# Crossbar transposes of K and Q issued one loop slot earlier, and stores held back for Pool's queue, in a window attention followed by a max-of-three FFN

## The chip, the cores and the metric

The kernel runs on one NeuronCore of a Trainium2 chip. The metric is the device time of one launch in microseconds. TensorE (PE) does the matmuls, VectorE (DVE), ScalarE (ACT) and GpSimd (POOL) the elementwise work, and SyncE (SP) issues most DMAs. Each engine takes its own instructions in order; so does each queue of DMA issues, SP's and Pool's among them.

## The reference

Attention over 4 batches × 8 heads × 768 positions × 64 dims: each query sees the first 4 positions (the sinks) and the last 128. Then an FFN with the elementwise maximum of three products.

```python
scores = scale * np.matmul(q, k.transpose(0, 1, 3, 2))
keep = is_sink | in_window              # n_sink = 4, window = 128
scores = np.where(keep, scores, -1e9)
a = softmax(scores)
x = np.matmul(a, v).transpose(0, 2, 1, 3).reshape(B * S, H * D)      # 3072 x 512
h = np.maximum(np.maximum(x @ w1, x @ w2), x @ w3)                   # 512 -> 768
out = h @ w_out                                                      # 768 -> 512, float32
```

## The kernel before

The work is cut into 12 chunks of 256 positions, three to a batch (c = 0, 1, 2 within it). For every chunk the kernel goes through these steps:

- **load**: three DMAs of 512 KB each (k, q, v in float32) on SP's queue, `load` (L74 to L80), into `raw` buffers of which there are 3 per tensor;
- **cast** (L488): Pool casts k and q to bfloat16 (`k_bf`, `q_bf`, two buffers each; L178) and v into `vb` (L181, four buffers);
- **transposition of K and Q**: for chunks 2 and 3 by TensorE and a copy out of PSUM (`turn`, L205), from chunk 4 on by the DMA crossbar (`turn_xbar`, L214: two DMAs for K at L217, one for Q at L220), issued on SP's queue; chunks 0 and 1 are transposed from float32 (`turn32`, L193). Results are `kT` and `qT`;
- **scores** (L516): sink scores (L254) and window scores (L279) on TensorE, exponentials on ACT (L281), masks on DVE (L287, L289);
- **attend** (L504): scores times V on TensorE (L311), normalised by DVE into `x_sb` (L317, L318), and then transposed to `xT`: by TensorE for chunks below 4 (`xpose`, L328), from then on by the crossbar with two DMAs on SP's queue (`xpose_xbar`, L337);
- **F** (`ffn_h`, L346): nine steps of 8 matmuls each (L352), copied by ACT (L356) or merged by DVE's maximum (L358);
- **y** (`ffn_y`, L360): two halves of 6 matmuls (L363), a copy by ACT (L369), and two stores each on SP's queue (L371).

The order on every engine is written out by hand. After a prologue and two slots written out (from L384 on), slot i of the loop at L574 runs, in this order: attend(i+1) with its x transposes, the casts of chunk i+2, the load of chunk i+3, four steps of F(i), the crossbar transposes of K and Q of chunk i+2, its scores, y(i−1) with its stores, the rest of F(i) between the masks. A transposition thus stands in the same slot as the scores that read it, and on SP's queue it stands behind x of chunk i+1 and the load of chunk i+3. PSUM has 8 banks that are taken in turn. The weights come in float32 and are cast by DMAs on Pool's queue (L147, L156).

Of the kernel before, what the change touches and what calls it, by code (L numbers as in the profile page):

```python
# [14 lines left out]
def kernel(  # L15
# [33 lines left out]
    KQ_XBAR = 4  # L49
    X_XBAR = 4  # L50

    with tc.manual_schedule():
# [21 lines left out]
        def load(ci, parts):  # L74
            b, c = divmod(ci, CPB)
            for t, g in parts:
                h = slice(0, H) if g is None else slice(4 * g, 4 * g + 4)
                nc.sync.dma_start(  # L78
                    out=raws[ci][t][:, h],
                    in_=dram[t][b, h, c * 256:c * 256 + 256].rearrange("h (p i) d -> p h (i d)", i=2))  # L80

        HALVES = [("k", 0), ("q", 0), ("k", 1), ("q", 1), ("v", 0), ("v", 1)]
        for ci in (0, 1):
            load_begin(ci)
            load(ci, HALVES)
# [25 lines left out]
        vb = [const.tile([128, 2, H, D + 1], BF16, name=f"vb{s}") for s in range(4)]  # L111
# [17 lines left out]
        def consts_late(eng):  # L129
            for s in range(1, 4):  # L130
                eng.memset(vb[s][:, :, :, D:D + 1], 1.0)
            for s in range(2):
                eng.memset(ks[s], 0.0)
            eng.memset(sel, 0.0)
            for h in range(2):
                for i in range(2):
                    eng.tensor_copy(sel[:, h, 4 * h + 2 * i:4 * h + 2 * i + 2],
                                    ident[:, 64 * i:64 * i + 2])
# [41 lines left out]
        def cast_v(ci, n, i, eng):  # L180
            eng.tensor_copy(vb[ci % 4][64 * i:64 * i + 64, n, :, 0:D],  # L181
                            raws[ci]["v"][64 * n:64 * n + 64, :, i])
# [49 lines left out]
        def sink_v(b, eng):  # L232
            t = bank([128, 2, D + 1], F32, "vs_ps")
            for p in range(NP):
                for h in range(2):
                    nc.tensor.matmul(t[32 * p:32 * p + 32, h], lhsT=sel[:, h],
                                     rhs=vb[(CPB * b) % 4][:, 0, 2 * p + h],
                                     start=(h == 0), stop=(h == 1), skip_group_check=True)
            eng(vs[b % 2], t)
# [53 lines left out]
        def av(ci, pairs, eng=None):  # L293
# [10 lines left out]
            for p in pairs:  # L304
                first = c == 0
                for t in range(2):
                    for s, n in ((2 * t, 2 * c + t - 1), (2 * t + 1, 2 * c + t)):
                        if n < 0:
                            continue
                        for h in range(2):  # L310
                            nc.tensor.matmul(  # L311
                                o[p][:, t, h], lhsT=es[ci, p][:, h, s],
                                rhs=vb[(CPB * b + n // 2) % 4][:, n % 2, 2 * p + h],
# [9 lines left out]
        def xT_of(ci):  # L323
            if ci not in xTs:
                xTs[ci] = work.tile([128, DS, 256], BF16, tag="xT", name="xT")
            return xTs[ci]

        def xpose(ci, g, eng):  # L328
            pt = bank([128, 2, 2, 128], BF16, "xt_ps")
            x = xs[ci].rearrange("p t h d -> p t (h d)")  # L330
            for a in range(2):
                for t in range(2):
                    ds = 2 * g + a
                    nc.tensor.transpose(pt[:, a, t], x[:, t, ds * 128:(ds + 1) * 128], ident)
            eng(xT_of(ci)[:, 2 * g:2 * g + 2], pt.rearrange("p a t c -> p a (t c)"))  # L335

        def xpose_xbar(ci):  # L337
            for t in range(2):
                nc.sync.dma_start_transpose(  # L339
                    out=xT_of(ci)[:, :, t * 128:(t + 1) * 128],  # L340
                    in_=xs[ci][:, t].rearrange("p h d -> p (h d)"))
# [4 lines left out]
        def ffn_h(ci, wi, fp):  # L346
# [3 lines left out]
            for f in range(2):  # L350
                for ds in range(DS):
                    nc.tensor.matmul(hp[:, f], lhsT=w_sb[wi, 2 * fp + f][:, ds],  # L352
                                     rhs=xTs[ci][:, ds], start=(ds == 0), stop=(ds == DS - 1))
# [5 lines left out]

        def ffn_y(ci, t, last=False):  # L360
# [4 lines left out]
            y = work.tile([128, d_model], F32, tag="y", bufs=4, name="y_sb")  # L365
            r0 = ci * 256 + t * 128
            o = out[r0:r0 + 128].rearrange("(r i) f -> i r f", i=2)
            if not last:
                nc.scalar.copy(y, yp)  # L369
                for i in range(2):  # L370
                    nc.sync.dma_start(out=o[i], in_=y[64 * i:64 * i + 64])  # L371
                return
            for i in range(2):
                ip = slice(64 * i, 64 * i + 64)
                if i:
                    nc.vector.tensor_copy(y[ip], yp[ip])
                else:
                    nc.scalar.copy(y[ip], yp[ip])
                (nc.sync, nc.scalar)[i].dma_start(out=o[i], in_=y[ip])

        V, P, A = nc.vector, nc.gpsimd, nc.scalar


        consts_dve()  # L384
        warm(8)
        turn32(0, "k", 0, V.tensor_copy)
        turn32(0, "q", 0, A.copy)
        warm(2)
        score(0, 0)
        turn32(0, "k", 1, V.tensor_copy)  # L390
        score(0, 1)
        turn32(0, "q", 1, A.copy)
        for n in range(2):
            for i in range(2):
                cast_v(0, n, i, P)
        mask(0, 0, V)
        score(0, 2)
        mask(0, 1, V)
        wait_for(raws[1]["k"][0:1, 0, 0, 0:1], P)
        load_w(0, 0, 256)  # L400
        load_w(0, 256, 256)
        load_w(0, 512, 256)
        load_w(1, 0, 256)
        turn32(1, "k", 0, V.tensor_copy)
        score(0, 3)
        turn32(1, "q", 0, V.tensor_copy)
        av(0, [0])
        mask(0, 2, V)
        av(0, [1])
        xpose(0, 0, A.copy)  # L410
        mask(0, 3, V)
        av(0, [2])
        turn32(1, "k", 1, V.tensor_copy)
        av(0, [3])
        turn32(1, "q", 1, V.tensor_copy)
        score(1, 0)
# [10 lines left out]
        mask(1, 0, V)  # L427
        ffn_h(0, 0, 0)
        score(1, 1)
        mask(1, 1, V)  # L430
# [4 lines left out]
        mask(1, 2, V)  # L435
# [3 lines left out]
        mask(1, 3, V)  # L439
        ffn_h(0, 1, 0)  # L440
        av(1, [2, 3])
        ffn_h(0, 1, 1)
        xpose(1, 0, A.copy)
        xpose(1, 1, A.copy)
        ffn_h(0, 1, 2)

        load_begin(2)
        wait_for(wts[2, 0][0:1, 0, 0:1], P)
        gate(2, "kqv", P)
        load(2, [("k", None), ("q", None), ("v", None)])  # L450
        for a in range(2):
            load_wo(a)
        for fp in range(3):
            ffn_h(1, 0, fp)
        cast_qk(2, "k", 0, P)
        cast_qk(2, "k", 1, P)
        for fp in range(3):
            ffn_h(1, 1, fp)
        for i in range(2):
            for n in range(2):  # L460
                cast_v(2, n, i, P)
        ffn_h(0, 2, 0)
        ffn_h(0, 2, 1)
        ffn_h(0, 2, 2)
        cast_qk(2, "q", 0, V)
        cast_qk(2, "q", 1, V)
        ffn_h(1, 2, 0)
        turn(2, "k", V.tensor_copy)
        turn(2, "q", A.copy)
        ffn_h(1, 2, 1)  # L470
        sink_score(2)
        for p in range(NP):
            score(2, p)
        ffn_h(1, 2, 2)
        load_begin(3)
        gate(3, "kqv", P)
        load(3, [("k", None), ("q", None), ("v", None)])
        for p in range(NP):
            mask(2, p, V)
        ffn_y(0, 0)  # L480
        ffn_y(0, 1)
        av(2, range(NP))
        ffn_y(1, 0)
        xpose(2, 0, A.copy)
        xpose(2, 1, A.copy)
        ffn_y(1, 1)

        def cast(ci):  # L488
            for t in "kq":
                for i in range(2):  # L490
                    cast_qk(ci, t, i, P)
            for n in range(2):
                for i in range(2):
                    cast_v(ci, n, i, P)

        def load_all(ci):
            if ci < NCH:
                load_begin(ci)
                load(ci, [("k", None), ("q", None), ("v", None)])

        def F(ci, n):
            ffn_h(ci, n % 3, n // 3)

        def attend(ci):  # L504
            if ci >= NCH:
                return
            av(ci, range(NP))
            if ci >= X_XBAR:
                xpose_xbar(ci)

        def T(ci):
            if ci < X_XBAR:
                xpose(ci, 0, A.copy)
                xpose(ci, 1, A.copy)

        def scores(ci):  # L516
            if ci >= NCH:
                return
            b, c = divmod(ci, CPB)
            if ci < KQ_XBAR:  # L520
                turn(ci, "k", V.tensor_copy)
                turn(ci, "q", A.copy)
            if c == 0:
                sink_k(b, V)
                sink_v(b, V.tensor_copy)
            sink_score(ci)
            for p in range(NP):
                score(ci, p)

        def masks(ci, ps_):  # L530
            for p in ps_:
                if ci < NCH:
                    mask(ci, p, V)


        cast(3)
        load_all(4)
        for n in range(5):
            F(2, n)
        scores(3)  # L540
        cast(4)
        load_all(5)
        turn_xbar(4)
        F(2, 5)
        masks(3, [0, 1])
        F(2, 6)
        masks(3, [2, 3])
        F(2, 7)
        F(2, 8)

        attend(3)
        ffn_y(2, 0)
        T(3)
        ffn_y(2, 1)
        cast(5)
        load_all(6)
        turn_xbar(5)
        scores(4)
        for n in range(3):
            F(3, n)  # L560
            masks(4, [n])
        F(3, 3)
        masks(4, [3])
        F(3, 4)
        attend(4)
        F(3, 5)
        F(3, 6)
        scores(5)
        F(3, 7)
        masks(5, [0, 1])  # L570
        F(3, 8)
        masks(5, [2, 3])

        for i in range(4, NCH):  # L574
            attend(i + 1)
            if i + 2 < NCH:
                cast(i + 2)
            load_all(i + 3)
            for n in range(4):
                F(i, n)  # L580
            if i + 2 < NCH:
                turn_xbar(i + 2)
            scores(i + 2)
            ffn_y(i - 1, 0)
            masks(i + 2, [0])
            ffn_y(i - 1, 1)
            masks(i + 2, [1])
            F(i, 4)
            masks(i + 2, [2])
            F(i, 5)  # L590
            masks(i + 2, [3])
            F(i, 6)
            F(i, 7)
            F(i, 8)
        ffn_y(NCH - 1, 0)
        ffn_y(NCH - 1, 1, last=True)
# [38 lines left out]
```

## Time and profile before

| | us |
|---|---|
| median of 3 runs | 271.96 (270.34 to 273.59) |
| the profiled execution | 271.53 |
| its span, first to last instruction | 269.6 |
| TensorE busy | 186.8 |
| VectorE, ScalarE, Pool busy | 115.1, 90.8, 64.3 |
| DMA packets of SP's queue, Pool's queue | 52.3%, 8.1% of 16 engines over the span |
| bytes moved | 34.92 MB |

How to read it: "busy" is the sum of the durations of an engine's instructions; the page also cuts the span into 40 slices and gives the busy share of each as a digit (9 is 90% or more), and beside it the granted TensorE clock in tenths. In the views, a line like `L217 SPq DMA_TRANSPOSE kT<-k_bf` is source line, queue or engine, operation, output and input. The chain of waits follows the last instruction back to what released each step. A wait in square brackets is the idle time of the engine before an instruction, and what ended it. Releasers are inferred from the times of the semaphores.

### The profile page before, as it was taken

The numbers are of one execution on the slowest core, as the hardware profiler recorded it, in microseconds if no ns is written. First come the engines' busy times: TensorE is split into PE (matmuls) and PEld (weight loads), VectorE is DVE, ScalarE is ACT, GpSimd is POOL, SyncE is SP. The second block draws the span as 40 slices with busy tenths as digits, with TensorE's granted clock in tenths as the row PEclk, the third lists the DMA queues.
The fourth block names the chain that finished last, engine by engine and source line by source line (L and its number), as shares of the span: only waits on it lengthen the run. The fifth ranks groups of instructions, "written<-read, shape, count | busy, mean of one in ns | idle before, by whom it ended". The sixth has DMA issues, their size and how long they took to land.

```text
span 269.6 us, 4874 instructions
## 1 busy us (share of the span) xinstructions
PE 186.8 (69%) x1934; PEld 138.2 (51%) x1946; DVE 115.1 (43%) x251; ACT 90.8 (34%) x177; POOL 64.3 (24%) x130
## 2 busy tenths in 40 slices
PE   6878999987777605940894099219903990999992
PEld 5665786774565503830483058115802580587870
DVE  4385676458186502640273028113800380283441
ACT  1528308453727105210711081015202510812221
POOL 3592223647351033005200510070015000000000
PEclk9999999999999965995599579757975798699998
DMA  6999974999892293339033903692187116034133
GB/s 185 278 147 189 199 178 122 251 264 245 216 232 43 47 254 50 80 67 282 4 78 82 270 2 78 162 190 48 38 197 148 45 40 113 0 80 93 26 78 79
DMA packets 71750, 34.92 MB, mean 130 GB/s; under 512 B 27440, under 2 KB 68656, under 8 KB 71728
## 3 DMA queue, kind: packets, MB, share of 16 engines
q1 hardware_dynamic: 67152, 31.34, 52.3%
q0 software_dynamic: 4496, 3.15, 8.1%
q8 instruction: 15, 0.25, 0.4%
q10 hardware_dynamic: 80, 0.13, 0.2%
q14 instruction: 7, 0.06, 0.1%
HBM read 25.17 MB, written 6.29 MB: 117 GB/s over the span
## 4 chain that ended last, share of the span: by engine, by line
PE 54%; DMA 25%; SPq 6%; DVE 5%; ACT 5%; issue 3%; POOL 1%; ACTq 0%; DVEq 0%; POOLq 0%
PE h_ps L352 27%; DMA q_raw<-in_q_dram 14%; PE y_ps L363 13%; DMA qT<-q_bf 10%; PE st L279 5%; SPq L339 4%; PE o_ps L311 3%; ACT e_sb L281 3%; PE kt L200 2%; PE qt L200 2%; DVE e_sb L287 2%; DVE h_sb L358 1%; DMA k_raw<-in_k_dram 1%; SPq L78 1%; SPq L217 1%
## 5 line engine op out<-in xcount | busy, mean ns | idle before, releaser
L352 PE MATMUL h_ps<-xT,w 128*128 128x256 bf16 x864 | 99.1, 273 | 1.2 <-ACT xT L335 1.1
L352 PEld LDWEIGHTS <-w 128*128 128x128 bf16 x864 | 83.5, 98 | 13.4 <-issue 2.1
L358 DVE TENSOR_TENSOR h_sb<-h_sb,h_ps 128x512 bf16<-128x512 bf16 x72 | 49.4, 686 | 54.8 <-PE h_ps L352 47.2
L281 ACT ACTIVATE e_sb<-st 128x512 bf16<-128x512 f32 (+1 forms) x96 | 45.6, 586 | 27.3 <-PE st L279 26.9
L287 DVE TENSOR_TENSOR e_sb<-e_sb,msk 128x1024 bf16<-128x1024 bf16 x32 | 21.8, 696 | 58.1 <-ACT e_sb L281 58.0
L356 ACT CAST h_sb<-h_ps 128x512 bf16<-128x512 f32 x36 | 21.2, 593 | 66.6 <-PE h_ps L352 66.6
L363 PE MATMUL y_ps<-wo,h_sb 128*128 128x512 bf16 x132 | 39.4, 438 | 1.8 <-issue 1.3
L178 POOL CAST k_bf<-k_raw 128x512 bf16<-128x512 f32 x20 | 11.9, 622 | 112.8 <-DMA k_raw<-in_k_dram 97.4
L181 POOL CAST vb<-v_raw 64x512 bf16<-64x512 f32 x48 | 30.5, 636 | 18.3 <-DMA v_raw<-in_v_dram 16.3
L279 PE MATMUL st<-qT,kT 64*128 64x128 bf16 (+1 forms) x256 | 17.7, 293 | 24.1 <-DMA qT<-q_bf 22.2
L254 PE MATMUL sk<-qT,ks 128*32 128x256 bf16 x32 | 2.8, 335 | 42.7 <-DMA qT<-q_bf 42.5
L363 PEld LDWEIGHTS <-h_sb 128*128 128x128 bf16 x144 | 15.2, 112 | 21.9 <-issue 11.9
L279 PEld LDWEIGHTS <-kT 64*128 64x128 bf16 x256 | 11.8, 117 | 28.4 <-issue 26.2
L254 PEld LDWEIGHTS <-ks 128*32 128x32 bf16 x32 | 1.1, 96 | 44.8 <-issue 42.9
L318 DVE TENSOR_TENSOR x_sb<-o_ps,rc 128x256 bf16<-128x256 f32 x48 | 20.4, 424 | 1.6
L369 ACT COPY y_sb<-y_ps 128x512 f32<-128x512 f32 x23 | 13.6, 601 | 17.7 <-PE y_ps L363 13.2
L311 PE MATMUL o_ps<-vb,e_sb 128*128 128x65 bf16 x352 | 14.9, 194 | 3.3 <-DVE e_sb L287 2.8
L258 ACT ACTIVATE e_sink<-sk 128x256 bf16<-128x256 f32 x8 | 3.1, 385 | 41.6 <-PE sk L254 41.6
L311 PEld LDWEIGHTS <-e_sb 128*128 128x128 bf16 x352 | 12.4, 97 | 5.7 <-DVE e_sb L287 3.9
L178 POOL CAST q_bf<-q_raw 128x512 bf16<-128x512 f32 x18 | 10.8, 629 | 6.4 <-DMA q_raw<-in_q_dram 6.4
L289 DVE TENSOR_TENSOR e_sb<-e_sb,msk 128x768 bf16<-128x768 bf16 x16 | 10.1, 651 | 4.6 <-ACT e_sb L281 4.6
L228 DVE COPY ks<-kT 64x16 bf16<-64x16 bf16 x8 | 2.1, 256 | 20.0 <-DMA kT<-k_bf 19.9
(59 smaller groups left out, 79.5 us busy)
## 6 DMA issues: line engine op xcount, KB each, us to landing
out_dram<-y_sb SPq DMA_DIRECT2D x47, 128.0 KB, 2.4
k_raw<-in_k_dram SPq DMA_DIRECT2D x10, 512.0 KB, 4.6
q_raw<-in_q_dram SPq DMA_DIRECT2D x10, 512.0 KB, 5.8
v_raw<-in_v_dram SPq DMA_DIRECT2D x10, 512.0 KB, 7.1
w<-in_moe_w_dram POOLq DMA_DIRECT2D x5, 256.0 KB, 5.6
k_raw<-in_k_dram SPq DMA_DIRECT2D x4, 256.0 KB, 5.2
q_raw<-in_q_dram SPq DMA_DIRECT2D x4, 256.0 KB, 5.3
v_raw<-in_v_dram SPq DMA_DIRECT2D x4, 256.0 KB, 5.4
```

The source lines that it names most:

```text
L178: eng.tensor_copy(bfs[ci, t][:, :, i], x)
L181: eng.tensor_copy(vb[ci % 4][64 * i:64 * i + 64, n, :, 0:D], raws[ci]["v"][64 * n:64 * n + 64, :, i])
L279: nc.tensor.matmul(o, lhsT=kk, rhs=qq, start=True, stop=True)
L281: nc.scalar.activation(e[:, h, lo:], st[h][:, lo:], AF.Exp, scale=scale)
L287: eng.tensor_mul(e, e, msk)
L311: nc.tensor.matmul(o[p][:, t, h], lhsT=es[ci, p][:, h, s], rhs=vb[(CPB * b + n // 2) % 4][:, n % 2, 2 * p + h], start=first, stop=(s == 2 ...
L318: nc.vector.tensor_mul(xs[ci][:, :, 2 * p:2 * p + 2], o[p][:, :, :, 0:D], rc.unsqueeze(3).to_broadcast([128, 2, 2, D]))
L352: nc.tensor.matmul(hp[:, f], lhsT=w_sb[wi, 2 * fp + f][:, ds], rhs=xTs[ci][:, ds], start=(ds == 0), stop=(ds == DS - 1))
L356: nc.scalar.copy(dst, hp)
L358: nc.vector.tensor_max(dst, dst, hp)
L363: nc.tensor.matmul(yp, lhsT=hs[ci][:, fb, t * 128:(t + 1) * 128], rhs=wo[fb // 3][:, fb % 3], start=(fb == 0), stop=(fb == FB - 1))
L369: nc.scalar.copy(y, yp)
```

## The change

- **K and Q a slot ahead.** In the loop, slot i now holds the cast of chunk i+3, the load of chunk i+4 and the transposition `KQ(i+3)`; the scores of chunk i+2 in that slot read what slot i−1 transposed. `vb` has five buffers instead of four. The slots before the loop are written out in the same manner.
- **Crossbar from chunk 5 on** (`KQ_XBAR`, `X_XBAR` 4 → 5): K, Q and x of chunk 4 are transposed by TensorE.
- **x in one DMA.** `xT` gets the layout half, block, column; one transposing DMA of 128 × 1024 takes the place of two. F reads its moving operand as two blocks of 128 columns.
- **y held.** y of a chunk is one tile of two halves, with 8 buffers instead of 4 tiles of one half. Nothing is stored before slot 7. From there Pool's queue stores, up to three chunks a slot: chunks 0 to 2, 3 to 5, 6 and 7, 8, 9. Chunk 10 and the first half of 11 go by SP, the last half by SP and ACT.
- **Prologue.** For chunk 0, two of the six half loads go by ACT's queue; v comes before the second halves of k and q. The first weights no longer wait for chunk 1's k. Load 2 waits for w2's first part instead of w3's; load 3 comes behind the cast of K of chunk 2, load 4 behind the casts of chunk 3 (`gated`: Pool writes one element of each raw tile first). 15 warming matmuls instead of 10. The steps of chunks 0 to 4 are interleaved anew.

The core of the diff:

```diff
-    KQ_XBAR = 4
-    X_XBAR = 4
+    KQ_XBAR = 5
+    X_XBAR = 5
...
-        HALVES = [("k", 0), ("q", 0), ("k", 1), ("q", 1), ("v", 0), ("v", 1)]
+        HALVES = [("k", 0), ("q", 0), ("v", 0), ("v", 1), ("k", 1), ("q", 1)]
         for ci in (0, 1):
             load_begin(ci)
-            load(ci, HALVES)
+            load(ci, HALVES, {("q", 0): nc.scalar, ("v", 1): nc.scalar} if ci == 0 else None)
...
         def xpose_xbar(ci):
-            for t in range(2):
-                nc.sync.dma_start_transpose(
-                    out=xT_of(ci)[:, :, t * 128:(t + 1) * 128],
-                    in_=xs[ci][:, t].rearrange("p h d -> p (h d)"))
+            nc.sync.dma_start_transpose(
+                out=xT_of(ci).rearrange("p t s c -> p (t s) c"),
+                in_=xs[ci].rearrange("p t h d -> p (t h d)"))
...
+        def store(ci, t, i, eng):
+            r0 = ci * 256 + t * 128
+            eng.dma_start(out=out[r0:r0 + 128].rearrange("(r i) f -> i r f", i=2)[i],
+                          in_=ys[ci][64 * i:64 * i + 64, t])
...
+        def KQ(ci):
+            if ci < NCH:
+                if ci < KQ_XBAR:
+                    turn(ci, "k", V.tensor_copy)
+                    turn(ci, "q", A.copy)
+                else:
+                    turn_xbar(ci)
...
-        warm(8)
+        warm(12)
...
-        wait_for(raws[1]["k"][0:1, 0, 0, 0:1], P)
...
-        wait_for(wts[2, 0][0:1, 0, 0:1], P)
+        wait_for(wts[1, 0][0:1, 0, 0:1], P)
...
-        for i in range(4, NCH):
-            attend(i + 1)
-            if i + 2 < NCH:
-                cast(i + 2)
-            load_all(i + 3)
+        held = 0
+        for i in range(5, NCH):
+            A_(i + 1)
+            if i + 1 < NCH:
+                xpose_xbar(i + 1)
+            cast(i + 3)
+            load_all(i + 4)
+            KQ(i + 3)
             for n in range(4):
                 F(i, n)
-            if i + 2 < NCH:
-                turn_xbar(i + 2)
             scores(i + 2)
-            ffn_y(i - 1, 0)
-            masks(i + 2, [0])
-            ffn_y(i - 1, 1)
-            masks(i + 2, [1])
+            late = i - 1 > 4
+            if late:
+                ffn_y(i - 1, 0)
+            masks(i + 2, 0)
+            if late:
+                ffn_y(i - 1, 1)
+            masks(i + 2, 1)
+            if i >= 7:
+                n = min(i - 1, held + 3) if i < NCH - 1 else i - 1
+                stores(range(held, n), P)
+                held = n
             F(i, 4)
...
+        stores(range(held, NCH - 1), nc.sync)
         ffn_y(NCH - 1, 0)
+        for i in range(2):
+            store(NCH - 1, 0, i, nc.sync)
         ffn_y(NCH - 1, 1, last=True)
```

## The prediction

> **What bounds the kernel now.** I read the page first: busy shares, then the slices.
>
> ```profile
> span 269.6 us, 4874 instructions
> PE 186.8 (69%) x1934; PEld 138.2 (51%) x1946; DVE 115.1 (43%) x251; ACT 90.8 (34%) x177; POOL 64.3 (24%) x130
> PE   6878999987777605940894099219903990999992
> PEclk9999999999999965995599579757975798699998
> ```
>
> TensorE is busy most, yet in the second half its row falls to 0 in a regular beat, and the granted clock falls with it. So one thing is missing once per slot of the loop; the view of waits names it.
>
> ```profile
> PE sk L254 <- DMA qT<-q_bf: 42.5, 6, 11.6
> PE st L279 <- DMA qT<-q_bf: 22.2, 2, 11.4
> 69.95 0.29 PE L254 MATMUL sk<-qT,ks 128*32 128x256 bf16 x4 [1.38 <-DMA qT<-q_bf]
> ```
>
> Columns: waiter, releaser, total us, times, longest. Eight waits, 64.7 us together, one for each of chunks 4 to 11, whose K and Q are transposed by the crossbar; the first, at 69.95, is still short, those from chunk 6 on are long. Why so late? SP's queue, Pool's casts and the chain over one slot (i = 6, from the views in order of time):
>
> ```profile
> 123.45 1.17 POOL L178 CAST k_bf<-k_raw 128x512 bf16<-128x512 f32 x2 [19.55 <-DMA k_raw<-in_k_dram]
> 125.16 1.17 POOL L178 CAST q_bf<-q_raw 128x512 bf16<-128x512 f32 x2 [0.55 <-DMA q_raw<-in_q_dram]
> 142.80 2.54 SPq L339 DMA_TRANSPOSE xT<-x_sb  x2
> 145.39 0.58 SPq L78 DMA_DIRECT2D k_raw<-in_k_dram  x1
> 146.02 5.57 DMA q_raw<-in_q_dram
> 147.85 3.85 SPq L217 DMA_TRANSPOSE kT<-k_bf  x2
> 151.80 1.34 SPq L220 DMA_TRANSPOSE qT<-q_bf  x1
> 155.28 0.41 PE sk L254 x3
> ```
>
> Counting loads from the start, the one at 145.39 is chunk 9's, and the transposes at 147.85 are chunk 8's, whose bf16 operands Pool had ready by 126.3. So the data was there 21 us early; what comes late is the issue, because on SP's in-order queue it stands behind x of chunk 7 (released at 142.80) and behind a load. The chain of waits puts 146.02 to 151.6 down to the landing of a q_raw; by the count that load is another chunk's. The last slot proves it: no load and no cast is left, and the wait is still there.
>
> ```profile
> 221.03 2.52 SPq L339 DMA_TRANSPOSE xT<-x_sb  x2
> 223.64 2.54 SPq L217 DMA_TRANSPOSE kT<-k_bf  x2
> 226.27 1.26 SPq L220 DMA_TRANSPOSE qT<-q_bf  x1
> 229.52 0.40 PE L254 MATMUL sk<-qT,ks 128*32 128x256 bf16 x4 [6.65 <-DMA qT<-q_bf]
> ```
>
> From x's release to the scores it takes 8.5 us without a load and 12.5 with one (142.80 to 155.28), while TensorE has four steps of F, about 3.5 us, to put beside it.
>
> **The change, part by part.** *K and Q one slot ahead.* The transposes of chunk i+3 now stand in slot i and are read in slot i+1. They still follow x and a load on SP, so they land some 12.5 us into slot i, and scores(i+3) come one slot plus 3.5 us in. With a slot of 13 us (below) that leaves 4 us; the waits go entirely. Their operands need cast(i+3), of a load issued at the head of slot i−1: the load lands in 5.6 us (146.02) and Pool has 5.4 us of work a chunk (64.3 / 12), 11 of 13 us, so SP doesn't stand there. Were it to stand, x of the next chunk and its load stand behind it. The price is one more slot of buffers (vb from 4 to 5); raw, kT and qT are freed two slots before reuse.
>
> What is late next? TensorE's own work, so I price it at full clock, from rows of the chain and of the order of time:
>
> ```profile
> 42.03 0.29 PE sk L254 x4
> 42.33 0.99 PE st L279 x24
> 46.96 0.23 PE o_ps L302 x8
> 47.18 1.10 PE o_ps L311 x32
> 49.58 0.62 PE xt_ps L334 x8
> 51.49 4.38 PE h_ps L352 x40
> 244.48 0.21 PE y_ps L363
> 244.74 2.32 PE y_ps L363 x10
> 247.07 7.86 PE h_ps L352 x72
> 264.65 0.59 ACT y_sb L378
> ```
>
> A chunk's F is 72 matmuls, 7.86; its two y 2.53 each pair (0.21 + 2.32); scores 0.29 + 0.99; attention times V 0.23 + 1.10. A full slot: 7.86 + 2.53 + 1.28 + 1.33 = 13.0 us, where the chain above shows 25 to 27. F(2, 0) begins at 51.49. What TensorE still has to do from there, after the change: F and y of chunks 2 to 11, 10 × 10.39 = 103.9; scores and AV of chunks 3 to 11, 9 × 2.61 = 23.5; x of chunks 3 and 4, 2 × 0.62; K and Q of chunks 3 and 4, 16 matmuls each.
>
> ```profile
> 40.37 0.58 PE qt L211 x7
> 128.90:134.00 5.10, 4.88 (x35) 2.46 (x37) 1.38 (x2) 4.50 (x10) 0.63 (x2) 0.50 0.01 3
> 0.00:30.00 30.00, 24.06 (x310) 17.79 (x311) 17.54 (x47) 13.15 (x26) 16.12 (x46) 1.00 1.02 194
> 30.00:51.50 21.50, 21.07 (x222) 16.07 (x224) 13.04 (x26) 10.48 (x20) 6.45 (x16) 1.00 0.82 193
> 145.30:155.30 10.00, 0.02 (x4) 0.05 (x4) 0.00 (x0) 0.00 (x0) 4.00 (x7) 0.64 0.97 223
> 160.70:165.00 4.30, 4.30 (x46) 3.68 (x45) 3.18 (x5) 1.18 (x3) 0.00 (x0) 1.00 0.53 122
> 221.00:223.60 2.60, 1.87 (x18) 1.43 (x15) 1.38 (x2) 0.59 (x1) 0.00 (x0) 1.00 0.27 53
> ```
>
> (The windows: stretch, length, PE, PEld, DVE, ACT, POOL busy, granted clock, DMA share, GB/s.) K and Q at 0.58 twice is 1.16 a chunk, 2.3. Together 130.9 us.
>
> *The clock.* After a wait of 11 us the next 5 us run at 0.50; 21.5 us without such a wait run at 1.00 (the windows at 128.90 and 30.00). Using full-clock prices already takes this gain: scores, y and the first F took 4.88 us there for what costs 2.5 to 3 at full clock, so about 2 us a slot.
>
> *Chunk 4 moved from crossbar to TensorE*: counted above; three transposes and two of x leave the DMA engines. The copies go to DVE and ACT, which have 9.6 and 7.6 us of work a chunk (115.1 and 90.8 / 12) beside 13.
>
> *x in one DMA.* Two issues of 1.26 become one. I take qT's row (the same 128 × 1024, 1.26 to issue, 3.1 to land) against 1.26 + 2.5 for two: no gain on the path, and F(i+1) reads it a slot later anyway. F's moving operand becomes two blocks of 128 instead of one of 256. The trace has no such F; the nearest, the sink scores, read Q in strides at 0.29 for four: I take nothing, with 5% of 94 us, 5 us, as the upper end.
>
> *y held, stored late by Pool.* A slot's load, K and Q take 9.7 us of DMA (0.97 × 10.0), x 0.7, the stores of two y 2.3 (0.53 × 4.3): 12.7 us of 13. Holding the stores back until slot 7 leaves 10.4, so the transfers fit. From slot 7 on come 3, 3, 2, 1, 1 chunks of stores: 40 DMAs on Pool's queue. In slot 7 that is 9.7 + 0.7 + 6.9 = 17.3 us of transfers, over 13; K and Q of chunk 10 can land 4 us late there, which eats the margin and no more. Pool's price for an issue:
>
> ```profile
> L147 POOL DMA_DIRECT2D w<-in_moe_w_dram x7 | 5.4, 778 | 0.0
> out_dram<-y_sb SPq DMA_DIRECT2D x47, 128.0 KB, 2.4
> 10.00:20.00 10.00, 7.72 (x128) 6.01 (x127) 7.64 (x17) 3.88 (x9) 9.63 (x23) 1.00 1.13 186
> 35.91 1.16 POOL L178 CAST k_bf<-k_raw 128x512 bf16<-128x512 f32 x2 [7.06 <-DMA k_raw<-in_k_dram]
> ```
>
> 0.78 us, 31 us in all, beside the casts of two more chunks, 10: Pool is done 41 us after slot 7 begins, at about 121 (50, two chunks of 14.8 with K, Q and x on TensorE, three of 13.0, 2.4 of stalls), long before the end. Lower end: nothing, as Pool is idle then; upper end: double the row, 1.6, when it would end at 195 and just touch the tail. I take the row: it was measured with DVE busy 7.64 of 10 us. The Trainium skill (SBUF — State Buffer, "A bandwidth-pool intuition that's wrong") speaks against Pool here: a DMA issued by GpSimd beside a DVE copy that holds the shared port takes about 3.1 us instead of 0.62. By it, 40 stores would be 124 us (an estimate from that page); the row shows no such thing beside this kernel's mix of DVE work.
>
> *Prologue.* k and q halves on two queues, v before the second halves, weights not waiting for chunk 1's k, load 2 released by an earlier weight, 5 more warming matmuls. TensorE is already busy 21.1 of the 21.5 us from 30 to 51.5, and 24.1 of the first 30: hardly more than 4 us can go, and weights ahead of chunk 1's loads could cost as much. I take F(2, 0) at 50, 1.5 earlier, with 47.5 and 54 as ends. Gates now chain load 3 behind K's cast of chunk 2 (35.91 before, not later after) and load 4 behind the casts of chunk 3: 35.9 + 1.2 + 5.6 + 5.4 + 5.6 = 53.7, so K of chunk 4 is cast at about 55 and turned at 65.
>
> *The tail* keeps its form: from the last y copy, 264.65, to the end, 5.0.
>
> **Sum.** 50 + 130.9 + 4 for short stalls (scores behind the Q copy of chunks 3 and 4, x of chunk 4 just before its transposition, 0.2 to 0.3 a slot elsewhere) + 5.0 = 189.9 span. The profiled execution took 271.53 for a span of 269.6, 1.9 more: 191.8; the median of the three runs is 0.4 above that one: **192**. Ends: 47.5 + 130.9 + 1.5 + 5 + 2.3 = 187; 54 + 130.9 + 7 + 5 + 2.3 = 199, both with the strided F at nothing.
>
> **Rivals.**
> 1. *The transfers come late after all.* For: 10.4 of 13 us a slot, over in slot 7, and the transposes still stand behind a load; the margin is 4 us. Against: stretches at 223 GB/s with share 0.97 carried a load and K and Q in 10 us. If they land in 20 instead of 12.5 us, five chunks (7 to 11) wait 3.5 each, 17 us: 209; with half of that, 201. A wait of 1.38 us (69.95) left the clock's slices at 9, one of 6.65 did not; waits of 3.5 lie between, and a halved clock would add up to 2 us each. The Trainium skill (TensorE: Matmul & The Clock Gate, "What's actually happening") has the clock halve after an idle window of 3.4 us: by it the 3.5 would pay and the halves not.
> 2. *The change doesn't do what it says*: SP reaches the transposes no earlier, because cast(i+3) or x holds it, and the waits stay. Against: casts 21 us early. Then 268.
> 3. *Pool's descriptors blocked by DVE.* The mechanism: every issue costs several times the row, and the 24 stores ahead of and behind cast(11) delay K and Q of chunk 11 as well as the end. At 2.5 us: 121 + 10 + 100 + 2.4 + 2.3 = 236. The Trainium skill's 3.1 us is this rival's rule (SBUF — State Buffer, same section).
> 4. *Slower: the same place at a higher price.* Pool's end passes the old time from (272 − 121 − 10 − 4.7) / 40 = 3.4 us an issue; at 3.7 it is 284. The row of 0.78 is four times away.
>
> **How the numbers follow.** Forecast (TensorE the bound): 0.66, own range 187 to 199. Transfers late: 0.24, 199 to 219. No effect: 0.03. Pool at 2 to 3.3 us: 0.05, 216 to 268. Slower: 0.02. The range 187 to 210 takes the forecast whole and most of rival 1. A measurement here tells about 1% (the three runs span 270.3 to 273.6). Faster by over 1%: all but rivals 2 (half) and 4: 0.96; within 1% 0.02; slower 0.02.
>
> **What would show it.** Waits on qT near zero, in place of 64.7; granted clock 1.00 from 90 us on; slots of 13 to 14 us; TensorE busy over 90% from 50 us; SP's L217 issued more than 10 us before its scores; Pool issuing stores at 0.8 us from about 121 and quiet before 175. Wrong it would be if scores wait for qT or F for xT in slots 7 and 8, if F's matmuls grow beyond 0.109 us each, or if F(2, 0) starts after 54.

## The result, and the profile after

The changed kernel takes 196.6 us (median of 4 runs, 195.67 to 198.08) against 272.4 before: 0.723 of the time, interval 0.716 to 0.729. The forecast was 192, with 187 to 210 as its range. Ratios, here and below, take only the executions within 1.5% of the shortest of their kernel. The profiled execution of the changed kernel has a span of 194.6. Line numbers from here on are those of the changed kernel: the scores are L280 and L255, K's transposition L218, Q's L221, Pool's stores L380, y L365.

From its page:

```profile
span 194.6 us, 4908 instructions
PE 176.9 (91%) x1963; PEld 135.3 (70%) x1975; DVE 115.1 (59%) x250; ACT 92.3 (47%) x182; POOL 89.2 (46%) x176
PE   6988989999997998898899999999589999999990
PEclk9999999999999999999999999999969999999998
DMA  5999999912999991002979949599999623231224
```

The zeros in TensorE's row are gone but for the last slice, which is the tail, and so are the dips of the clock: one 5 is left in the slice from 136 to 141 us, and the one 6 of the clock stands in the slice after it. TensorE's busy time fell by 10 us, although it has more to do (chunk 4): that is the halved clock (0.87 granted on average before, 0.99 after). Y's matmuls take 33.4 us instead of 39.4 and the window scores 14.2 instead of 17.7; both stand right behind the old waits.

The longest waits of TensorE after the start-up (waiter, releaser, total us, times, longest):

```profile
PE sk L255 <- DMA qT<-q_bf: 2.9, 1, 2.9
PE o_ps L312 <- DVE e_sb L290: 2.2, 4, 0.9
PE o_ps L312 <- DVE e_sb L288: 1.1, 2, 0.6
PE xt_ps L335 <- DVE x_sb L319: 1.0, 4, 0.3
```

64.7 us on qT in eight waits became 2.9 in one. The chain, from F(2, 0) to TensorE's last matmul:

```profile
48.81 3.49 PE h_ps L352 x32
...
187.51 2.43 PE y_ps L365 x10
189.97 0.59 ACT y_sb L375
```

TensorE's queue in order of time, over slots 7 and 8, shows a full slot and then the one that stalls:

```profile
121.71 1.17 PE L312 MATMUL o_ps<-vb,e_sb 128*128 128x65 bf16 x32
122.72 3.65 PE L352 MATMUL h_ps<-xT,w 128*128 128x256 bf16 x32
126.49 0.88 PE L280 MATMUL st<-qT,kT 64*128 64x256 bf16 x16
127.45 2.75 PE L365 MATMUL y_ps<-wo,h_sb 128*128 128x512 bf16 x11
130.04 4.53 PE L352 MATMUL h_ps<-xT,w 128*128 128x256 bf16 x40
134.41 0.91 PE L312 MATMUL o_ps<-vb,e_sb 128*128 128x65 bf16 x24
135.15 3.65 PE L352 MATMUL h_ps<-xT,w 128*128 128x256 bf16 x32
141.70 0.29 PE L255 MATMUL sk<-qT,ks 128*32 128x256 bf16 x4 [2.89 <-DMA qT<-q_bf]
141.92 1.89 PE L280 MATMUL st<-qT,kT 64*128 64x128 bf16 x24
144.57 2.70 PE L365 MATMUL y_ps<-wo,h_sb 128*128 128x512 bf16 x10 [0.22 <-issue]
```

From F(7, 0) at 122.72 to F(8, 0) at 135.15 a slot takes 12.4 us: one step behind the other, as priced. Then the scores of chunk 10 wait 2.89 us, and run at half clock after it (24 matmuls in 1.89 instead of about 1.0). SP's and Pool's queues say why:

```profile
120.97 1.26 SPq L221 DMA_TRANSPOSE qT<-q_bf  x1
124.61 1.24 SPq L339 DMA_TRANSPOSE xT<-x_sb  x1
127.28 3.17 SPq L79 DMA_DIRECT2D v_raw<-in_v_dram  x1
130.55 5.12 SPq L218 DMA_TRANSPOSE kT<-k_bf  x2
135.78 1.94 SPq L221 DMA_TRANSPOSE qT<-q_bf  x1
124.53 4.75 POOL L380 DMA_DIRECT2D out_dram<-y_sb  x9
135.78 5.79 DMA qT<-q_bf
```

(The last line is the chain's.) Nine of the twelve stores are in the POOL line, and three more are issued by 131.8. Load 11 and K and Q of chunk 10 are issued while twelve stores run on Pool's queue. K's two issues take 5.12 us, Q lands 5.8 us after its issue, at 141.6, 17.0 us after x's issue at 124.61. The prediction had 12.5 and, in this slot, 4 more.

### The profile page after: what moved, and what is told of

The parts are those of the page before. It is cut to its first block, busy times and chain, and to the rows that moved or that the text cites. A ratio compares the mean times of both kernels' runs of the same rounds, so it can differ in the third digit from the quotient of the medians.

```text
span 194.6 us, 4908 instructions
## 1 busy us (share of the span) xinstructions
PE 176.9 (91%) x1963; PEld 135.3 (70%) x1975; DVE 115.1 (59%) x250; ACT 92.3 (47%) x182; POOL 89.2 (46%) x176
## 4 chain that ended last, share of the span: by engine, by line
PE 66%; DVE 11%; DMA 10%; ACT 8%; issue 3%; SPq 1%; DVEq 0%; ACTq 0%; POOLq 0%
PE h_ps L352 37%; PE y_ps L365 14%; ACT e_sb L282 5%; DMA q_raw<-in_q_dram 5%; PE o_ps L312 5%; PE st L280 4%; DMA qT<-q_bf 3%; DVE h_sb L358 3%; DVE x_sb L319 3%; DVE e_sb L290 2%; DMA k_raw<-in_k_dram 2%; PE kt L201 2%; ACT qT L192 1%; PE xt_ps L335 1%; PE qt L201 1%
## 5 line engine op out<-in xcount | busy, mean ns | idle before, releaser
L352 PEld LDWEIGHTS <-w 128*128 128x128 bf16 x864 | 83.4, 98 | 12.9 <-issue 1.5
L182 POOL CAST vb<-v_raw 64x512 bf16<-64x512 f32 x48 | 32.7, 681 | 10.1 <-DMA v_raw<-in_v_dram 8.2
L365 PE MATMUL y_ps<-wo,h_sb 128*128 128x512 bf16 x132 | 33.4, 384 | 2.0 <-DVE h_sb L358 0.7
L288 DVE TENSOR_TENSOR e_sb<-e_sb,msk 128x1024 bf16<-128x1024 bf16 x32 | 24.0, 755 | 15.8 <-ACT e_sb L282 15.7
L380 POOL DMA_DIRECT2D out_dram<-y_sb x40 | 21.0, 531 | 20.3 <-ACT y_sb L371 17.7
L365 PEld LDWEIGHTS <-h_sb 128*128 128x128 bf16 x144 | 13.8, 99 | 16.8 <-issue 2.0
L371 ACT COPY y_sb<-y_ps 128x512 f32<-128x512 f32 x23 | 13.6, 629 | 17.6 <-PE y_ps L365 17.6
L280 PE MATMUL st<-qT,kT 64*128 64x128 bf16 (+1 forms) x256 | 14.2, 247 | 0.7 <-DVE h_sb L358 0.3
L280 PEld LDWEIGHTS <-kT 64*128 64x128 bf16 x256 | 9.7, 98 | 3.6 <-issue 1.5
L336 ACT COPY xT<-xt_ps 128x512 bf16<-128x512 bf16 x10 | 5.7, 594 | 9.8 <-PE xt_ps L335 9.8
L318 DVE RECIPROCAL rc<-o_ps 128x4 f32<-128x4 f32 x48 | 8.3, 174 | 3.1 <-PE o_ps L312 3.1
L335 PE MATMUL xt_ps<-ident,x_sb 128*128 128x128 bf16 x40 | 4.4, 221 | 1.1 <-DVE x_sb L319 1.0
```

The source lines that it names most:

```text
L182: eng.tensor_copy(vb[ci % 5][64 * i:64 * i + 64, n, :, 0:D], raws[ci]["v"][64 * n:64 * n + 64, :, i])
L280: nc.tensor.matmul(o, lhsT=kk, rhs=qq, start=True, stop=True)
L288: eng.tensor_mul(e, e, msk)
L352: nc.tensor.matmul(hp[:, f].rearrange("p (t c) -> p t c", t=2), lhsT=w_sb[wi, 2 * fp + f][:, ds], rhs=xTs[ci][:, :, ds], start=(ds == 0), ...
L365: nc.tensor.matmul(yp, lhsT=hs[ci][:, fb, t * 128:(t + 1) * 128], rhs=wo[fb // 3][:, fb % 3], start=(fb == 0), stop=(fb == FB - 1))
L380: eng.dma_start(out=out[r0:r0 + 128].rearrange("(r i) f -> i r f", i=2)[i], in_=ys[ci][64 * i:64 * i + 64, t])
```

## The experiments

Theory A: the gain is that K and Q are issued a slot early; with the wait goes the halved clock. Theory A on the rest: the one wait left comes from stores, load, K and Q meeting in slot 7. Rivals: the transfers fill the slots, so that the held stores are needed (B); the new order of the early chunks and the held stores bring much by themselves (C). Ratios are to the kernel before, run on the same chip.

**K and Q ahead alone, in the kernel before.**

```diff
         for i in range(4, NCH):
             attend(i + 1)
-            if i + 2 < NCH:
-                cast(i + 2)
             load_all(i + 3)
+            if i + 3 < NCH:
+                cast(i + 3)
             for n in range(4):
                 F(i, n)
-            if i + 2 < NCH:
-                turn_xbar(i + 2)
             scores(i + 2)
+            if i + 3 < NCH:
+                turn_xbar(i + 3)
```

(Cast and transposition of chunk 6 stand ahead of the loop.)

> The kernel before with one edit: K and Q of chunk i+3 are cast and transposed in slot i, after the scores of i+2; stores at once, two x DMAs, crossbar from chunk 4 on and the old prologue stay. Theory A (the late issue of K and Q is the whole matter): the six long waits of 6.7 to 11.6 us (62 in all) and about 2 us of halved clock behind each go, 272.4 - 62 - 12 = 198, 196 to 204 with small waits left. Rival B (the transfers need the stores out of the way: 12.7 of 13 us of DMA a slot): waits of 2 to 4 us on qT stay in most slots, 212 or more.

211.9 us, 0.778 (0.775 to 0.782): 60 of the 75 us, but above A's range and right at the lower end of B's; the waits that are left, seven of up to 4.0 us, look like B's too. The waits, and SP's queue in one slot with Pool's cast in it:

```profile
PE sk L254 <- DMA qT<-q_bf: 11.0, 6, 4.0
PE st L279 <- DMA qT<-q_bf: 1.9, 1, 1.9
109.23 0.58 SPq L78 DMA_DIRECT2D k_raw<-in_k_dram  x1
111.40 0.58 SPq L78 DMA_DIRECT2D v_raw<-in_v_dram  x1
113.76 1.17 POOL L178 CAST k_bf<-k_raw 128x512 bf16<-128x512 f32 x2 [7.83 <-issue]
114.95 2.52 SPq L217 DMA_TRANSPOSE kT<-k_bf  x2
```

From 112.0 to 114.95 SP stands: K's transposition waits for the cast (113.76 to 114.93) of the load that was issued in the same slot. Neither A nor B had said that; the load must be a slot ahead too.

**K, Q and the load ahead.** As above, but the load of chunk i+4 stands in slot i, `turn_xbar(i + 3)` right behind it, and `vb` has five buffers.

> The kernel before with K and Q one slot ahead and the load one slot ahead as well (load of i+4, cast and transposition of i+3 in slot i, vb five buffers); stores at once, two x DMAs, crossbar from chunk 4 on and the old prologue stay. In the run with K and Q ahead alone the transposition stood for the cast of a load of the same slot, and 13 us of waits were left. If that missing lead is the cause, the waits fall under 5 us: 200 to 204. Rival (the second x DMA and stores at once on SP keep them): 208 to 212.

202.3 us as the median of six executions from 199.2 to 203.9. The ratio, 0.735 (0.730 to 0.740), goes by the three shortest; all six would give 0.743. The waits on qT are down to 3.4 us in four. So the lead of load, cast and transposition is worth 70 to 72 of the 75 us, with stores at once, two x DMAs and the old prologue. B falls.

**K and Q put back in the changed kernel.**

```diff
-            KQ(i + 3)
             for n in range(4):
                 F(i, n)
+            KQ(i + 2)
             scores(i + 2)
```

(And K and Q of chunks 6 and 7 likewise.)

> The changed kernel with K and Q of chunks 6 to 11 put back right before the scores that read them; everything else (held stores, one x DMA, prologue, chunk 4 on TensorE) stays. Theory A: six waits of about 10 us (one x DMA takes 1.3 off the 11.4) plus 2 us of clock come back, 196.6 + 72 - 5 = 264, 255 to 270. Rival C (held stores and the new order of the early chunks bring much of the gain): under 235.

247.5 us, 0.908 (0.902 to 0.914): most of the gain goes, but 17 us less than A expected, and below its range.

```profile
PE sk L255 <- DMA qT<-q_bf: 29.4, 4, 9.5
PE st L280 <- DMA qT<-q_bf: 15.0, 2, 8.6
```

Six waits come back, 44.4 us in all instead of 60. The three with a load in front of K and Q on SP are 8.6 to 9.5; the three without one (chunk 6, and the last two, since the loads run a slot ahead) 6.45, 5.6 and 5.0. So the load ahead helps K and Q even when they are not ahead themselves: chunks 6 and 10, which have no load in front of them here, wait 5 and 6 us less than in the kernel before, where they had one (11.42 and 11.60). C is ruled out at its number (235), but 25 us of the old cost does hang on the rest of the change.

**y stored at once by SP, in the changed kernel.** `ffn_y` stores each half after its copy, `stores` is left out.

> The changed kernel, but every half of y is stored at once by SP's queue as before. Theory A: K and Q have a slot to land, the stores are hidden, and the one wait of 2.9 us for chunk 10, which I put down to Pool's burst of stores in slot 7, goes with its 2 us of clock: 192 to 197. Rival B (transfers fill the slots): waits on qT in slots 5 to 8, 203 or more.

196.4 us, 0.721 (0.718 to 0.725): no difference to holding them. The wait for chunk 10 is gone, and two others have come, of 3.30 us for chunk 6 and 1.66 for chunk 8. Holding the stores, as the change does it, gains nothing. The wait for chunk 6 has a cause that SP's queue shows, first here and then in the changed kernel:

```profile
83.76 2.41 SPq L382 DMA_DIRECT2D out_dram<-y_sb  x4
86.28 3.39 SPq L218 DMA_TRANSPOSE kT<-k_bf  x2
66.21 3.46 SPq L218 DMA_TRANSPOSE kT<-k_bf  x2
```

SP issues nothing from 78.8 to 83.76, until y of chunk 3 is copied (ACT's copies at 83.04, L371). K of chunk 6 stands behind these stores, and is issued 20 us later than in the changed kernel. What delayed chunk 8 was not traced.

**The same late stores by SP's queue instead of Pool's.**

```diff
-                stores(range(held, n), P)
+                stores(range(held, n), nc.sync)
```

> The changed kernel with the late stores in the same slots, but issued by SP's queue in place of Pool's. If the wait for chunk 10 comes from Pool's stores sharing the DMA engines with K and Q that were issued after them, it goes, because SP issues the stores behind K and Q: 191 to 193. Rival (slot 7 has more transfers than it holds, whatever the queue; or x of the next chunk now stands behind 12 issues of 0.6 us): 196 to 200, with a wait on qT or xT.

192.5 us, 0.707 (0.704 to 0.710), so 4 us better than the changed kernel, and as much better than with stores at once on the same queue. SP's queue in slot 7:

```profile
125.39 1.23 SPq L339 DMA_TRANSPOSE xT<-x_sb  x1
129.49 3.47 SPq L218 DMA_TRANSPOSE kT<-k_bf  x2
133.05 1.25 SPq L221 DMA_TRANSPOSE qT<-q_bf  x1
134.35 7.99 SPq L380 DMA_DIRECT2D out_dram<-y_sb  x12
```

The same twelve stores now stand behind K and Q in one queue: K's issues are back to 3.47 us, and no wait on qT is left. Holding the stores does gain, then, if SP issues them behind K and Q.

**Stores spread, by Pool.** The stretch of 78 to 90 us is free of transfers, because load 8 stands behind x of chunk 5 on SP. From the windows of the changed kernel and then of this one (stretch, length, PE, PEld, DVE, ACT, POOL, clock, DMA share, GB/s):

```profile
78.00:90.00 12.00, 11.31 (x139) 8.10 (x140) 7.83 (x19) 7.42 (x15) 1.12 (x2) 1.00 0.01 3
78.00:90.00 12.00, 11.04 (x132) 7.80 (x132) 7.80 (x21) 7.42 (x15) 7.06 (x14) 1.00 0.45 134
```

```diff
         cast(7)
+        stores(range(0, 3), P)
         load_all(8)
...
-                n = min(i - 1, held + 3) if i < NCH - 1 else i - 1
+                n = min(i - 1, held + (1 if i == 7 else 3)) if i < NCH - 1 else i - 1
```

(And `held` starts at 3.)

> The changed kernel, Pool still stores, but y of chunks 0 to 2 goes out behind the casts of chunk 7, in the stretch from 76 to 90 us in which the DMA share is 0.01; one chunk of stores in slot 7 and three in slot 8 are left. Theory A (the wait for chunk 10 comes from 12 stores in slot 7 beside a load, K and Q): the wait of 2.9 us and 2 us of halved clock go, 191 to 193. Rival (Pool's queue delays K and Q wherever its stores lie): the wait moves to another slot, 195 to 198.

192.3 us, 0.704 (0.701 to 0.708), without a wait on qT. Twelve stores by Pool still stand in slot 8 here, beside K and Q of chunk 11, but no load is left there, and they delay nobody.

**The load ahead of x on SP's queue,** the burst of stores unchanged.

```diff
             A_(i + 1)
+            load_all(i + 4)
             if i + 1 < NCH:
                 xpose_xbar(i + 1)
             cast(i + 3)
-            load_all(i + 4)
```

(Load 8, ahead of the loop, likewise.)

> The changed kernel with the load of a slot issued ahead of x on SP's queue, so that it doesn't stand behind the end of attention; nothing else moved, Pool's burst of 12 stores in slot 7 stays. Theory A': K and Q of chunk 10 come late because they are queued behind load 11, which x of chunk 8 holds back; with the load issued a dozen us sooner they need x alone, the wait goes, 191 to 193. Rival (the burst alone is enough, wherever the load lies): a wait of 2 us or more for chunk 10 or 11, 195 to 198.

192.7 us, 0.706 (0.703 to 0.709), no wait on qT either. Load 11 goes out at 118.62 instead of 125.90:

```profile
118.62 0.57 SPq L79 DMA_DIRECT2D k_raw<-in_k_dram  x1
125.21 1.42 SPq L339 DMA_TRANSPOSE xT<-x_sb  x1
126.73 3.39 SPq L218 DMA_TRANSPOSE kT<-k_bf  x2
130.21 1.26 SPq L221 DMA_TRANSPOSE qT<-q_bf  x1
```

Q of chunk 10 is issued 5.6 us sooner. So the wait takes both: twelve stores on another queue beside K and Q, and a load in front of them that x has held back. Taking either away removes it, and its 4 to 5 us.

**x by two DMAs in the changed kernel.** `xpose_xbar` with a loop over the halves, as before.

> The changed kernel with x transposed by two DMAs of 128 x 512 instead of one of 128 x 1024. By the prediction x has a slot of slack, so one DMA gains nothing by itself: 196 to 198, with the wait for chunk 10 about 1.3 us longer (the second issue stands ahead of load, K and Q). Rival (one transposing DMA is much cheaper, or F waits for x): over 201, with waits on xT.

199.1 us, 0.729 (0.727 to 0.732): 1.7 us slower, a little above what was expected, and the interval touches that of the changed kernel (0.716 to 0.729). The waits on qT are 1.48 and 4.25, the latter 1.4 longer than the 2.89, as expected; none is on xT. So all that the single DMA shows by itself is SP's 1.26 us ahead of K and Q.

**The old prologue in the changed kernel.**

```diff
-            load(ci, HALVES, {("q", 0): nc.scalar, ("v", 1): nc.scalar} if ci == 0 else None)
+            load(ci, HALVES)
...
-        wait_for(wts[1, 0][0:1, 0, 0:1], P)
+        wait_for(wts[2, 0][0:1, 0, 0:1], P)
```

(and the lines from the first warming matmul to x of chunk 1 as before).

> The changed kernel with the prologue of before, up to the transposition of x of chunk 1, its order of half loads on SP alone, and load 2 released by w3's first part again. F(2, 0) began at 51.5 before and 48.7 after; if the prologue is worth that and nothing is given back later, 199 to 200. Rival (later slots absorb it, as the transfers are the same): 196 to 197.

201.1 us, 0.736 (0.733 to 0.739): 3.5 us slower, about 1 us over what was expected; F(2, 0) begins at 51.6 instead of 48.8, and the wait for chunk 10 is 3.69.

**The changed prologue added to the kernel with K, Q and load ahead.**

> The kernel before with K, Q and load one slot ahead, and with the changed prologue too; stores at once, two x DMAs and the crossbar from chunk 4 on stay. If the parts add up, the prologue takes its 3 to 4 us from the 202.3 of the run without it: 198 to 200, one or two over the changed kernel. Rival (the gain of the prologue is given back while the early loads wait): 201 to 203. Either way the waits on qT should be short ones, under 5 us together.

201.1 us, 0.736 (0.731 to 0.740): by the ratios the same as without it, within intervals of half a per cent each, and by the medians of all six executions 1 us less. That is the rival's number: the parts do not add up. Its executions spread from 198.5 to 204.1, and the one in the profile is the 204.1; there the clock is lowered three times, at 76 and 88 us behind short waits for masks and late behind a wait of 2.63 us on qT (the first and the last of these):

```profile
76.00:80.00 4.00, 3.39 (x29) 2.53 (x30) 3.86 (x11) 0.00 (x0) 3.84 (x7) 0.66 1.02 178
148.90:152.00 3.10, 3.10 (x31) 1.84 (x32) 0.73 (x2) 2.52 (x6) 0.00 (x0) 0.50 0.67 173
```

Over the whole execution the granted clock was 0.999 in the shortest of the six and 0.970 in this one. That such drops, which come in one execution and not in another, eat what the prologue gained is likely, and not shown.

**The changed kernel once more, and the removals together** (load ahead of x, late stores on SP, K and Q of chunk 3 one step of F sooner, scores of chunk 5 between attention and x of chunk 4).

> The changed kernel unaltered, as the mark for the two others of this call on the same chip: 196 to 198.

> The changed kernel with the load ahead of x, the late stores on SP's queue, K and Q of chunk 3 turned one step of F sooner, and the scores of chunk 5 put between attention and x of chunk 4. Both ways of removing the wait for chunk 10 remove the same 5 us, so they don't add up: 192. The two reorderings take short waits on DVE (0.7 at 61, 0.6 at 76, 0.8 at 78): 190.5 to 191.5. Rival (these waits only move to the next bank or mask): 192 to 193.

197.2 us (0.723, 0.719 to 0.727) and 191.3 us (0.702, 0.699 to 0.706). The latter is the fastest version: 6 us better than the change. As expected, the ways to remove the wait do not add up. Of the short waits for masks about a third went, in its profile from 2.2 + 1.1 to 1.4 + 0.7, and one of 0.8 for Pool's cast of v came; the gain over the best single edit (0.704) is within the intervals.

## Why the prediction was right, and where it was short

**The cause.** Right, and shown from both sides: the issue was late, not the data. The step that read the last slot (a wait without any load) carried it; the chain's name for that time, a landing of q_raw, would have led to faster loads. That the load has to move too was in the change, and the prediction leaned on it where it said that SP won't stand for the cast; the run without it keeps 13 us of waits.

**The sum, term by term.** F(2, 0): 50 forecast, 48.8 measured. TensorE's work and stalls from there to its last matmul: 130.9 + 4 forecast, 141.1 measured (187.51 + 2.43 − 48.81). The tail: 5.0 and 4.7. So the term that was mis-sized is the stalls, 10.2 us instead of 4: 2.9 for chunk 10's wait, about 1.7 for the halved clock after it, 4.0 in short waits on DVE, and 1.6 that the profile doesn't put down to one cause. Without chunk 10's wait three kernels stand at 192.3 to 192.7: the forecast, to 1 us. That closeness is in part luck: with the late stores on SP, F(2, 0) begins at 48.9, 1.1 us early, and TensorE's work and stalls take 137.2 us, 2.3 more than forecast.

**The step that failed** is the margin in slot 7: "K and Q of chunk 10 can land 4 us late there, which eats the margin and no more". They did land 4.5 us late (17.0 against 12.5). But the margin wasn't 4 us: I counted the landing from x's issue, and the need from the start of the slot. DVE's normalisation lies between, 122.7 to 124.6, and slot 7 was 12.4 us, not 13.0, as it holds the scores of a chunk without sinks. The need came 14.2 us after x's issue (138.8), so 1.7 us were there. Rival 1 was thus right for one of its five chunks, and scores that wait for qT in slot 8 are what the prediction itself had named as a sign of being wrong.

**The clock.** The forecast that it would stay at 1.00 held but for that wait. By the Trainium skill (TensorE: Matmul & The Clock Gate, "What's actually happening") the clock halves after an idle window of about 3.4 us, so a wait of 2.9 us would not have paid. The runs differ from it. After 2.89 us of waiting the clock was 0.50 (first line); after 1.87 us in the run with K and Q ahead alone, with thin work around it, 0.50 too (second), while waits of 2.05 and 1.97 us in that run left it at 1.00; after 3.30 us in the run with stores at once it stayed 1.00 (third).

```profile
143.00:145.00 2.00, 1.78 (x15) 0.81 (x13) 0.97 (x2) 2.00 (x5) 2.00 (x5) 0.50 1.14 209
139.00:141.00 2.00, 2.00 (x6) 0.73 (x5) 0.56 (x1) 1.83 (x5) 0.00 (x0) 0.50 0.47 59
92.70:96.00 3.30, 3.11 (x36) 2.52 (x37) 0.56 (x1) 2.91 (x8) 0.00 (x0) 1.00 0.77 199
```

**Pool's stores.** The price was on the safe side:

```profile
L380 POOL DMA_DIRECT2D out_dram<-y_sb x40 | 21.0, 531 | 20.3 <-ACT y_sb L371 17.7
L352 PE MATMUL h_ps<-xT,w 128*128 128x256 bf16 x864 | 99.6, 273 | 0.7 <-DVE vs L240 0.5
```

0.53 us an issue against 0.78, first at 124.5, last at 174.4. The Trainium skill's 3.1 us beside DVE copies (SBUF — State Buffer, "A bandwidth-pool intuition that's wrong") doesn't show here: DVE was busy 8.7 of the 12.9 us from 121.5 to 134.4. Rivals 3 and 4 had no ground. What Pool's stores cost is not Pool's time but their place: in a queue of their own they run beside K and Q that were issued after them, and with a load in front as well these come late.

**F's strided operand** costs nothing: 273 ns a matmul before and after.

**The prologue** gave 2.7 us at F(2, 0), more than the 1.5 I took, 3.5 at the end of the changed kernel, and nothing clear of the spread without the rest.

## What to carry to other kernels

When an engine waits for a DMA, look for when its operands were ready and what stands ahead of its issue on the queue; a last iteration without the suspected transfer tells order from bandwidth. Moving a transfer a slot ahead means moving its whole chain, load and cast too. Transfers that nobody waits for belong behind the urgent ones in the same queue, or in a stretch without any; in another queue they run beside them and can delay them, and ahead of them in the same queue a store whose data isn't there yet holds them up.

## What the runs showed of the hardware

Waits of 1.9 us (with thin work around it) and 2.9 us were enough to halve TensorE's clock for 3 us or more, and waits of 2.0 and 3.3 us elsewhere were not; no length separates the two. So a short wait in a dense kernel costs either its own length or that and up to 2 us more. Stores of 128 KB on Pool's queue took a median of 4.3 us to land in the changed kernel, and 2.4 on SP's queue in the run with the late stores there. The two issues of K's transposition took 2.5 us on a free queue. Behind a load they took 3.5 to 3.8 in the changed kernel (4.9 once in the run with stores at once), and 5.1 behind a load with Pool's stores running.
